# A gated recurrence with a convolution-gated linear unit: stores on ScalarE's queue, five output buffers, two x buffers, and gated inputs of two chunks from PSUM

## The chip, the cores and the metric

The kernel runs on one core of one Trainium2 chip. A core has five engines with a queue each: PE (TensorE, matrix products and transposes), DVE (VectorE), ACT (ScalarE, activation functions), POOL (GpSimd) and SP (SyncE, which here issues transfers). They share the on-chip memory SBUF; PE writes its results to the eight banks of PSUM, which DVE and ACT read. Transfers between HBM and SBUF are issued by an engine's queue and carried out by 16 DMA engines.

Each engine works through its own instructions in order and waits on semaphores where an operand, or a buffer to be overwritten, belongs to another engine. The metric is the device time of one execution in microseconds (us). The rows of the profile come from one profiled execution.

## The reference

Four sequences of 6336 tokens with 256 channels, all float32. First a gated linear recurrence over the tokens, then a linear unit whose gate is a causal convolution of the recurrence's output:

```python
sig_r = 1 / (1 + exp(-r_gate));  sig_i = 1 / (1 + exp(-i_gate))
a_t = exp(8 * sig_r * log(clip(sigmoid(a_param), 1e-6, 1 - 1e-6)))
x_gated = sqrt(maximum(1 - a_t * a_t, 1e-6)) * sig_i * x
for t in range(S):
    h = a_t[:, t] * h + x_gated[:, t];  y[:, t] = h
gate = 1 / (1 + exp(-sum_k(conv_w[k] * y_shifted_by(4 - k))))   # 5 taps
out = (gate * (y @ w_val)) @ w_out
```

## The kernel before

All 25,344 tokens are treated as one long row, cut into 28 chunks (`CHUNKS`, line 16): 256, 512, then 23 of 1024, then 512, 256 and 256. For the second half of the work a chunk is cut again into parts of at most 512 tokens, of which there are 51. In the plan an operation is named by its kind and by numbers: `tanh.7` is the tanh of chunk 7; `exp.7.1` belongs to chunk 7 and channel half 1; `conv.7.1` to chunk 7 and token part 1. A last number is the PSUM bank.

A chunk passes these steps; the line is the one that the profile shows:

- `ldri`, `ldx` (SP, L221 and L225): load r_gate and i_gate, and x. A gate buffer holds one chunk's pair, and there are three (`NRI`); there are three x buffers (`NX`).
- `tanh` (ACT, L294): tanh of half of both gates, in place as bf16.
- `srT` (PE, L299), `exp` (ACT, L308): transpose to channels on partitions, then the decay a, written to one of five slots of `aring`.
- `e` (POOL, L314): a squared. `sq` (ACT, L344): the square root of a quarter of 1 - a², for up to three chunks at once.
- `s1` and `u` (POOL, L322 and L335): one plus the tanh of the input gate, in place, then times x. For chunks 0 to 3 (`U_DVE`) DVE does both in one instruction per 256 tokens instead (L332), with the gate and x in SBUF.
- `nT` (PE, L357), `xg` (DVE, L364), `xgT` (PE, L372): transpose the root back, multiply the gated input by it, and transpose the product.
- `scan` (DVE, L385): the recurrence along the tokens of one channel half, into `yring`, which holds three chunks.
- `conv` (PE, L397), `tg` (ACT, L407), `val` (PE, L415), `gv` (DVE, L420), `out` (PE, L429): convolution, its tanh, value product, gating, output product.
- `osbD` (DVE, L444) or `osbA` (ACT, L440): the output from PSUM to one of three output buffers (`NOSB`).
- `store` (SP, L449): the output buffer to HBM.

The square root needs another activation table than tanh and exp, so ACT loads tables (ACT_TABLE_LOAD); before the change these loads come with the activations by themselves. Kernel set-up (L238 to L272) turns `a_param` into a scale, with an exponential between two logarithms on ACT, and turns the convolution weights into columns. `wd` (DVE, L279 and L280) makes from them the diagonal matrices of `conv`, and `wc` (DVE, L287 and L288) casts the two weight matrices. Their float32 originals, which `ldw` loads in five transfers on SP, lie in the last slot of `aring` until they are cast; chunk 4's exp writes that slot next.

The order is written out by hand in one string, `PLAN`. A loop runs through it and emits each operation to its engine, so the string sets the order on every queue. The loads that stand ahead of the first other operation are emitted before the set-up. SP carries loads and stores in one order: a load that stands behind a store in the plan is issued after it. Waits are added where buffers are shared.

Of the kernel before, what the change touches and what calls it, by code (L numbers as in the profile page):

```python
# [8 lines left out]
P = 128  # L9
HP = 64  # L10
SUBN = 512
BANK = 512
# [3 lines left out]
CHUNKS = [256, 512, 1024, 1024, 1024, 1024, 1024, 1024, 1024, 1024, 1024, 1024, 1024, 1024, 1024, 1024, 1024, 1024, 1024, 1024, 1024, 1024, 1024, 1024, 1024, 512, 256, 256]  # L16
U_DVE = [0, 1, 2, 3]
NRI = 3
NX = 3
# [4 lines left out]
NOSB = 3  # L24
# [9 lines left out]
ldri.1.-1 ldx.0.-1 ldri.0.-1 ldx.1.-1 tanh.1.-1 ldri.2.-1 tanh.0.-1 srT.1.0.5 exp.1.0.-1 srT.0.1.4 u.0.-1 srT.0.0.1  # L34
exp.0.0.-1 e.1.0.-1 u.1.-1 exp.0.1.-1 srT.1.1.1 exp.1.1.-1 e.0.1.-1 e.0.0.-1 e.1.1.-1 sq.0.1.-1 ldri.3.-1 sq.1.1.-1
tanh.2.-1 nT.1.0.5 xg.1.0.-1 xgT.1.0.7 nT.0.0.0 xg.0.0.-1 ldri.4.-1 xgT.0.1.6 scan.0.1.-1 tanh.3.-1 srT.2.1.4
srT.2.0.1 xgT.1.1.5 xgT.0.0.2 scan.0.0.-1 scan.1.1.-1 ldx.2.-1 exp.2.0.-1 wd.-1 srT.3.0.2 srT.3.1.5 exp.2.1.-1
e.2.0.-1 scan.1.0.-1 exp.3.1.-1 ldx.4.-1 e.2.1.-1 exp.3.0.-1 conv.0.0.4 tanh.4.-1 u.2.-1 e.3.0.-1 ldw.-1 ldx.3.-1
e.3.1.-1 tg.0.0.-1 srT.4.0.7 wc.-1 exp.4.0.-1 s1.4.-1 ldri.5.-1 sq.2.2.-1 val.0.0.6 srT.4.1.2 gv.0.0.-1 e.4.0.-1
u.3.-1 out.0.0.0 u.4.-1 osbD.0.0.-1 exp.4.1.-1 ldri.6.-1 nT.2.0.6 nT.2.1.0 xg.2.0.-1 nT.3.0.6 nT.3.1.4 tanh.5.-1  # L40
e.4.1.-1 xg.2.1.-1 xg.3.0.-1 xgT.2.1.5 xg.3.1.-1 conv.1.0.2 scan.2.1.-1 ldx.5.-1 tg.1.0.-1 srT.5.1.6 s1.5.-1 xgT.2.0.4
exp.5.1.-1 xgT.3.1.1 scan.2.0.-1 val.1.0.2 tanh.6.-1 e.5.1.-1 ldri.7.-1 scan.3.1.-1 srT.5.0.4 u.5.-1 conv.2.0.6
exp.5.0.-1 srT.6.1.5 gv.1.0.-1 conv.2.1.0 tg.2.0.-1 srT.6.0.3 ldx.6.-1 tg.2.1.-1 xgT.3.0.2 e.5.0.-1 exp.6.1.-1
scan.3.0.-1 val.2.0.0 exp.6.0.-1 ldri.8.-1 e.6.1.-1 tanh.7.-1 gv.2.0.-1 val.3.0.2 conv.3.0.4 e.6.0.-1 out.2.0.0
val.2.1.6 s1.6.-1 tg.3.0.-1 osbD.2.0.-1 sq.4.3.-1 gv.3.0.-1 ldx.7.-1 out.1.0.0 s1.7.-1 conv.3.1.4 osbD.1.0.-1
gv.2.1.-1 u.6.-1 srT.7.0.0 store.0.0.-1 store.1.0.-1 out.2.1.2 ldx.8.-1 osbD.2.1.-1 exp.7.0.-1 nT.4.0.1 u.7.-1
nT.4.1.2 xg.4.0.-1 ldri.9.-1 nT.5.0.7 xg.4.1.-1 srT.7.1.3 nT.5.1.1 xg.5.0.-1 tg.3.1.-1 nT.6.0.6 xgT.4.0.0 exp.7.1.-1
xg.6.0.-1 out.3.0.4 xg.5.1.-1 tanh.8.-1 val.3.1.2 osbD.3.0.-1 e.7.1.-1 xgT.5.0.6 gv.3.1.-1 xgT.5.1.5 store.2.1.-1
e.7.0.-1 scan.4.0.-1 nT.6.1.2 ldri.10.-1 srT.8.1.4 tanh.9.-1 srT.8.0.3 s1.8.-1 xgT.4.1.7 xg.6.1.-1 scan.4.1.-1 u.8.-1
exp.8.0.-1 scan.5.0.-1 conv.4.0.0 exp.8.1.-1 store.2.0.-1 conv.4.1.2 tg.4.0.-1 scan.5.1.-1 store.3.0.-1 srT.9.1.7  # L50
e.8.0.-1 val.4.0.0 exp.9.1.-1 ldx.10.-1 srT.9.0.4 tg.4.1.-1 gv.4.0.-1 xgT.6.0.5 e.9.1.-1 out.3.1.6 exp.9.0.-1
scan.6.0.-1 out.4.0.2 tanh.10.-1 ldx.9.-1 e.8.1.-1 val.4.1.0 osbD.3.1.-1 conv.5.0.4 e.9.0.-1 osbD.4.0.-1 ldx.11.-1
tg.5.0.-1 val.5.0.2 s1.9.-1 sq.7.3.-1 xgT.6.1.7 gv.5.0.-1 val.5.1.4 store.4.0.-1 gv.4.1.-1 out.5.0.2 s1.10.-1
store.3.1.-1 scan.6.1.-1 out.4.1.0 ldri.11.-1 u.9.-1 osbD.4.1.-1 conv.5.1.6 osbD.5.0.-1 tg.5.1.-1 nT.7.1.1 nT.7.0.0
xg.7.1.-1 srT.10.0.2 u.10.-1 xg.7.0.-1 srT.10.1.1 ldri.12.-1 exp.10.0.-1 xgT.7.0.0 gv.5.1.-1 conv.6.0.6 exp.10.1.-1
scan.7.0.-1 out.5.1.2 tg.6.0.-1 nT.8.0.1 tanh.11.-1 val.6.0.4 e.10.0.-1 xg.8.0.-1 osbD.5.1.-1 conv.6.1.6 gv.6.0.-1
store.4.1.-1 xgT.7.1.2 e.10.1.-1 val.6.1.0 scan.7.1.-1 store.5.0.-1 tg.6.1.-1 srT.11.0.3 srT.11.1.5 s1.11.-1
# [433 lines left out]
```

## Time and profile before

| | |
|---|---|
| median of 7 runs | 313.14 us (311.3 to 314.56) |
| the profiled execution | 311.45 us, of which the span from first to last instruction is 309.7 |
| busy: ACT | 281.4 us (91% of the span) |
| busy: DVE | 266.2 us (86%) |
| busy: PE | 245.3 us (79%) |
| busy: POOL | 230.7 us (74%) |
| moved by DMA | 104.76 MB, 338 GB/s over the span |
| granted clock of TensorE | 0.998 |

Rows of groups that the change touches (count, mean of one):

| line | engine and operation | count | mean ns |
|---|---|---|---|
| L332 | DVE, gated input, 128x512 | 11 | 1703 |
| L335 | POOL, gated input, 128x2048 | 21 | 4143 |
| L322 | POOL, one plus the gate, 128x2048 | 21 | 1919 |
| L314 | POOL, a squared, 128x1024 | 46 | 1947 |
| L444 | DVE, output copy, 128x1024 | 37 | 1213 |
| L440 | ACT, output copy, 128x1024 | 11 | 1008 |
| all | ACT_TABLE_LOAD | 24 | 1283 |

Busy time is the time in which an engine executes; a row's mean is that of one instruction, and neighbours on an engine overlap a little, so that the means add up to slightly more than the busy time. "Idle before, releaser" in a row says how long the engine stood idle ahead of an instruction and what ended that. An idle engine costs something only where it sets the pace.

### The profile page before, as it was taken

How to read it: one execution, taken by the hardware profiler on the slowest of the kernel's cores; microseconds unless marked ns; L12 is line 12 of the kernel's file. 1: busy time of each engine (PE TensorE's matmuls, PEld its weight loads, DVE VectorE, ACT ScalarE, POOL GpSimd, SP SyncE). 2: the span in 40 equal slices, each digit the busy share in tenths (PEclk: the TensorE clock that was granted, in tenths of full speed). 3: DMA queues.
4: the chain of work that ended last, by engine and by line, in shares of the span. 5: the costliest groups of instructions: out<-in, count | busy, mean ns of one | idle time of the engine just before them, and what ended most of it. 6: DMA issues, size and time to landing. Idle time of an engine off the chain costs nothing.

```text
span 309.7 us, 6478 instructions
## 1 busy us (share of the span) xinstructions
PE 245.3 (79%) x2655; PEld 167.9 (54%) x2655; DVE 266.2 (86%) x221; ACT 281.4 (91%) x191; POOL 230.7 (74%) x116
## 2 busy tenths in 40 slices
PE   0256156878868898979997998899979988999992
PEld 0134125546645665556765674657666655666561
DVE  1328978868798999999999999999999999889982
ACT  6999396999999999999999999999999998898652
POOL 0405985799899999997999699889999995690000
PEclk9999999999999999999999999999999999999999
DMA  7999655998999999999999999999999968563255
GB/s 268 421 424 382 259 247 223 431 380 297 372 424 416 377 380 416 390 424 369 392 362 359 323 426 419 423 424 341 354 416 398 357 239 336 196 217 134 103 205 205
DMA packets 20075, 104.76 MB, mean 338 GB/s; under 512 B 2247, under 2 KB 2766, under 8 KB 11214
## 3 DMA queue, kind: packets, MB, share of 16 engines
q1 hardware_dynamic: 20032, 104.34, 86.3%
q8 instruction: 21, 0.34, 0.4%
q14 instruction: 8, 0.07, 0.1%
q10 hardware_dynamic: 14, 0.01, 0.0%
HBM read 78.39 MB, written 25.95 MB: 337 GB/s over the span
## 4 chain that ended last, share of the span: by engine, by line
ACT 30%; DVE 30%; PE 16%; issue 16%; DMA 4%; POOL 1%; ACTq 0%; SPq 0%; DVEq 0%
DVE yring L385 11%; DVE gvr L420 8%; ACT gate L294 8%; ACT aring L308 7%; DVE osb L444 6%; ACT ering L344 6%; PE pp L397 5%; ACT tgr L407 4%; DVE uring L364 4%; PE pp L429 3%; DMA gate<-in_i_gate_dram 3%; PE pp L415 3%; PE pp L372 2%; PE pp L357 2%; ACT L344 2%
## 5 line engine op out<-in xcount | busy, mean ns | idle before, releaser
L314 POOL TENSOR_TENSOR ering<-aring 128x1024 f32<-128x1024 f32 (+2 forms) x56 | 97.2, 1756 | 35.7 <-ACT aring L308 35.5
L385 DVE TENSOR_TENSOR_SCAN yring<-aring,yring,pp 128x1024 bf16<-128x1024 f32 (+2 forms) x54 | 114.7, 2139 | 4.1 <-PE pp L372 4.1
L335 POOL TENSOR_TENSOR uring<-gate,xr 128x2048 bf16<-128x2048 bf16 (+2 forms) x24 | 91.2, 3813 | 5.0 <-DMA xr<-in_x_dram 4.7
L294 ACT ACTIVATE gate<-gate 128x4096 bf16<-128x4096 f32 (+2 forms) x28 | 90.3, 3230 | 1.6 <-DMA gate<-in_i_gate_dram 1.3
L397 PE MATMUL pp<-yring,diag 64*64 64x512 bf16 (+15 forms) x1260 | 66.9, 337 | 6.7 <-DVE yring L385 3.0
L420 DVE SCALAR_TENSOR_TENSOR gvr<-tgr,pp 128x1024 bf16<-128x1024 bf16 (+1 forms) x51 | 59.5, 1177 | 6.7 <-PE pp L415 3.5
L308 ACT ACTIVATE aring<-pp,khf 128x1024 f32<-128x1024 bf16 (+2 forms) x56 | 60.3, 1115 | 5.4 <-issue 5.1
L415 PE MATMUL pp<-yring,wv 128*128 128x512 bf16 (+1 forms) x204 | 51.0, 375 | 10.1 <-DVE wv L287 4.2
L407 ACT ACTIVATE tgr<-pp 128x1024 bf16<-128x1024 f32 (+1 forms) x51 | 50.8, 1004 | 8.3 <-PE pp L397 8.1
L429 PE MATMUL pp<-wo,gvr 128*128 128x256 bf16 x396 | 51.7, 275 | 4.9 <-DVE yring L385 2.0
L397 PEld LDWEIGHTS <-diag 64*64 64x64 bf16 x1260 | 32.5, 107 | 32.8 <-issue 17.1
L429 PEld LDWEIGHTS <-gvr 128*128 128x128 bf16 x396 | 42.0, 114 | 14.7 <-issue 8.2
L444 DVE COPY osb<-pp 128x1024 f32<-128x1024 f32 (+1 forms) x38 | 44.8, 1198 | 4.6 <-PE pp L429 3.5
L322 POOL TENSOR_SCALAR gate<-gate 128x2048 bf16<-128x2048 bf16 (+2 forms) x24 | 42.4, 1774 | 7.1 <-ACT gate L294 7.1
L344 ACT ACTIVATE ering<-ering,b 128x4096 bf16<-128x4096 f32 (+4 forms) x16 | 46.4, 2932 | 0.2
L357 PE MATMUL pp<-ident_f,ering 128*128 128x128 f32 x198 | 33.2, 309 | 15.3 <-ACT ering L344 9.1
L299 PE MATMUL pp<-ident_b,gate 128*128 128x128 bf16 x396 | 32.4, 233 | 16.0 <-ACT gate L294 12.5
L364 DVE TENSOR_TENSOR uring<-uring,pp 128x1024 bf16<-128x1024 bf16 (+1 forms) x51 | 32.4, 663 | 9.1 <-PE pp L357 8.2
L299 PEld LDWEIGHTS <-gate 128*128 128x128 bf16 x396 | 26.6, 104 | 25.1 <-ACT gate L294 15.9
L357 PEld LDWEIGHTS pp<-ident_f,ering 128*128 128x128 f32 x198 | 27.9, 208 | 20.9 <-ACT ering L344 11.8
L372 PE MATMUL pp<-ident_f,uring 128*128 128x128 f32 x198 | 32.5, 287 | 2.5 <-DVE uring L364 1.9
L415 PEld LDWEIGHTS <-wv 128*128 128x128 bf16 x204 | 19.4, 98 | 27.1 <-issue 9.4
(36 smaller groups left out, 93.1 us busy)
## 6 DMA issues: line engine op xcount, KB each, us to landing
out_dram<-osb SPq DMA_DIRECT2D x48, 512.0 KB, 5.8
gate<-in_r_gate_dram SPq DMA_DIRECT2D x23, 1024.0 KB, 8.9
gate<-in_i_gate_dram SPq DMA_DIRECT2D x23, 1024.0 KB, 9.3
xr<-in_x_dram SPq DMA_DIRECT2D x23, 1024.0 KB, 12.2
gate<-in_r_gate_dram SPq DMA_DIRECT2D x2, 512.0 KB, 4.6
gate<-in_i_gate_dram SPq DMA_DIRECT2D x2, 512.0 KB, 4.2
xr<-in_x_dram SPq DMA_DIRECT2D x2, 512.0 KB, 5.8
xr<-in_x_dram SPq DMA_DIRECT2D x3, 256.0 KB, 4.3
```

What stands on the lines that cost most here:

```text
L294: nc.scalar.activation(out=tgate[:, s0:s0 + 2, 0:w], in_=gate[:, s0:s0 + 2, 0:w], func=ACT.Tanh, scale=0.5)
L308: nc.scalar.activation(out=dst, in_=src, func=ACT.Exp, scale=khf[:, h:h + 1], bias=khf[:, h:h + 1])
L314: nc.gpsimd.tensor_tensor(out=ering[:, c % NE, h * n:(h + 1) * n], in0=a, in1=a, op=ALU.mult)
L335: nc.gpsimd.tensor_tensor(out=u, in0=t, in1=xt, op=ALU.mult)
L344: nc.scalar.activation(out=nring[:, c % NE:c % NE + m, 0:w], in_=ering[:, c % NE:c % NE + m, 0:w], func=ACT.Sqrt, scale=-0.25, bias=b025[: ...
L357: nc.tensor.transpose(out=pp[:, d0:d0 + P], in_=src[:, w, :], identity=ident_f[:])
L385: nc.vector.tensor_tensor_scan(out=yring[:, h, y0:y0 + n], data0=aring[:, c % NA, h, 0:n], data1=src, initial=prev, op0=ALU.mult, op1=ALU.add)
L397: nc.tensor.matmul(out=pp[col * HP:(col + 1) * HP, b0 + d0:b0 + d1], lhsT=diag[r * HP:(r + 1) * HP, h, kk, :], rhs=yring[r * HP:(r + 1) * ...
L415: nc.tensor.matmul(out=pp[:, (bank + m) * BANK:(bank + m) * BANK + n], lhsT=wv[:, hk, m, :], rhs=yring[:, hk, y0:y0 + n], start=(hk == 0), ...
L420: nc.vector.scalar_tensor_tensor(out=gvr[:, nth[k] % NGV, :, 0:n], in0=tgr[:, nth[k] % NTG, :, 0:n], scalar=1.0, in1=two(live["val", k], n ...
L429: nc.tensor.matmul(out=pp[:, bank * BANK + j * D:bank * BANK + (j + 1) * D], lhsT=gvr[:, nth[k] % NGV, m, 0:n].rearrange("c (p q) -> c q p ...
L444: nc.vector.tensor_copy(out=dst, in_=src)
```

## The change

- Chunks: 512, 23 of 1024, then 512, 512 and 256: 27 chunks and 50 parts.
- Stores are issued by ACT's queue, at places that the new plan sets, and there are five output buffers. There are two x buffers instead of three.
- For chunks 0 and 1 (`X_PE`) PE multiplies x by an identity matrix in float32 and so puts it into PSUM, 256 tokens at a time (`xc`), and DVE makes the gated input from there (`ux`; `u` is the last of them). Chunks 2 and 3 get `s1` and `u` on POOL as the later ones do.
- The diagonal matrices are made on POOL in the set-up. The weight casts are three instructions on ACT. The raw weights lie in the third chunk slot of `yring`, come in three transfers and are loaded ahead of everything but the first gates and x. The order of channels in the gated product changes (`QUADS`), and with it the way the casts and the load of `w_out` lay out their columns.
- Activation tables are loaded by name: a table with logarithm and exponential at the start, then the exponential one, and after that whenever the next of tanh, exp, tg and sq needs the other.
- The plan is a new one: 11 `sq` as before, in other groups (0; 1 and 2; 3 to 5; ...), 41 copies on DVE and 9 on ACT.

```diff
-CHUNKS = [256, 512, 1024, ..., 1024, 512, 256, 256]
-U_DVE = [0, 1, 2, 3]
+CHUNKS = [512, 1024, ..., 1024, 512, 512, 256]
+X_PE = [0, 1]
-NX = 3
+NX = 2
-NOSB = 3
+NOSB = 5
...
+ldri.0.-1 ldri.1.-1 ldx.0.-1 ldx.1.-1 ldri.2.-1 ldw.-1 tanh.0.-1 srT.0.0.7 srT.0.1.5 exp.0.1.-1 exp.0.0.-1 e.0.0.-1
+tanh.1.-1 e.0.1.-1 xc.0.1.0 xc.0.0.6 ux.0.0.-1 xc.1.2.1 u.0.-1 sq.0.1.-1 ux.1.2.-1 srT.1.0.0 ldri.3.-1 xc.1.1.5
+ldx.2.-1 nT.0.0.7 srT.1.1.4 exp.1.0.-1 xg.0.0.-1 ux.1.1.-1 exp.1.1.-1 xc.1.0.0 tanh.2.-1 xc.1.3.5 e.1.1.-1 ux.1.0.-1
+e.1.0.-1 wc.-1 srT.2.0.3 s1.2.-1 srT.2.1.2 xgT.0.0.4 exp.2.0.-1 scan.0.0.-1 exp.2.1.-1 e.2.0.-1 u.1.-1 tanh.3.-1
...
-        wvf = aring[:, NA - 1, 0, 0:H * D].rearrange("p (h n) -> p h n", h=H)
-        wof = aring[:, NA - 1, 1, 0:H * D].rearrange("p (h n) -> p h n", h=H)
+        wvf = yring[:, 0, 2 * CMAX:3 * CMAX].bitcast(FP32).rearrange("p (h n) -> p h n", h=H)
+        wof = yring[:, 1, 2 * CMAX:3 * CMAX].bitcast(FP32).rearrange("p (h n) -> p h n", h=H)
...
-        nc.scalar.activation(out=kln[:, 0:1], in_=b025[:], func=ACT.Ln)
+        nc.scalar.preload_act_table_set("natural_log_exp_and_others")
...
+        nc.scalar.preload_act_table_set("exp_and_others")
...
-        def op_wd(k, bank):
-            nc.vector.tensor_tensor(out=id64[:], ...
+        nc.gpsimd.tensor_tensor(out=id64[:], in0=ident_f[:, 0:HP], in1=ident_f[:, HP:P], op=ALU.add)
+        nc.gpsimd.tensor_tensor(out=diag[:].rearrange("p h k m -> p (h k) m"), ...
...
         def op_wc(k, bank):
+            for hk in range(H):
+                nc.scalar.copy(out=wv[:, hk, :, :].rearrange("p m (i c) -> p i m c", i=2),
+                               in_=wvf[:, hk, :].rearrange("p (i m c) -> p i m c", i=2, m=2))
+            nc.scalar.activation(out=wo2[:], in_=wof, func=ACT.Copy, scale=0.5)
...
+        def op_xc(k, bank):
+            c, w = k
+            nc.tensor.matmul(out=pp[:, bank * BANK:(bank + 1) * BANK], lhsT=ident_f[:],
+                             rhs=xr[:, c % NX, 2 * w:2 * w + 2, :].rearrange("p b d -> p (b d)"),
+                             start=True, stop=True)
+
+        def op_ux(k, bank):
+            c, w = k
+            u, t = gated(c)
+            b = live["xc", k]
+            nc.vector.scalar_tensor_tensor(out=u[:, w], in0=t[:, w], scalar=1.0,
+                                           in1=pp[:, b * BANK:(b + 1) * BANK].rearrange("p (b d) -> p b d", b=2),
+                                           op0=ALU.add, op1=ALU.mult)
...
-        QUADS = ((0, 0, 0), (0, 1, 1), (1, 0, 1), (1, 1, 0))
+        QUADS = ((0, 0, 0), (0, 1, 1), (1, 1, 1), (1, 0, 0))
...
-            nc.sync.dma_start(toks(of, c, o, n),
-                              osb[:, nth[k] % NOSB, 0:n // P * D].rearrange("p (q d) -> p q d", d=D))
+            nc.scalar.dma_start(toks(of, c, o, n),
+                                osb[:, nth[k] % NOSB, 0:n // P * D].rearrange("p (q d) -> p q d", d=D))
...
+            if o[0] in ("tanh", "exp", "tg", "sq"):
+                want = "sqrt_and_others" if o[0] == "sq" else "exp_and_others"
+                if want != table:
+                    nc.scalar.preload_act_table_set(want)
+                table = want
```

On ACT the new plan begins `tanh.0 exp.0.1 exp.0.0 tanh.1 sq.0.1 exp.1.0 exp.1.1 tanh.2 wc exp.2.0 exp.2.1 tanh.3 sq.1.2 exp.3.1 tanh.4 tg.0.0 exp.3.0 exp.4.1 tanh.5 tg.1.0 exp.4.0 exp.5.1 exp.5.0 tanh.6 tg.1.1 store.0.0 tg.2.0 sq.3.3`, and ends `sq.25.2 tg.22.1 osbA.21.1 store.20.0 tg.23.1 store.21.1 tg.23.0 store.20.1 store.22.1 store.22.0 tg.24.0 osbA.23.0 store.23.1 tg.25.0 store.23.0 tg.26.0 store.24.0 osbA.25.0 store.25.0 osbA.26.0 store.26.0`.

## The prediction

> **What bounds the kernel now.** I first read the busy times by stretch (per engine: us busy, instructions; then the granted clock, the DMA share, GB/s).
>
> ```profile
> core 0: us, PE busy (x) PEld busy (x) DVE busy (x) ACT busy (x) POOL busy (x), PEclk, DMA share, GB/s
> 0.00:8.00 8.00, 0.60 (x3) 0.46 (x3) 1.02 (x7) 5.64 (x7) 0.70 (x6) 1.00 0.77 273
> 8.00:40.00 32.00, 12.36 (x86) 8.55 (x87) 19.19 (x20) 26.43 (x20) 15.85 (x9) 1.00 0.95 374
> 40.00:80.00 40.00, 29.17 (x310) 20.12 (x310) 31.44 (x26) 36.93 (x23) 34.14 (x13) 1.00 0.81 317
> 80.00:180.00 100.00, 88.22 (x961) 60.35 (x959) 96.85 (x74) 99.33 (x59) 92.86 (x43) 1.00 0.99 385
> 180.00:260.00 80.00, 71.10 (x783) 49.58 (x782) 78.81 (x61) 79.42 (x49) 73.07 (x34) 1.00 0.97 380
> 260.00:280.80 20.80, 20.65 (x235) 13.40 (x233) 18.40 (x16) 18.10 (x22) 14.05 (x12) 1.00 0.55 202
> 280.80:309.70 28.90, 23.22 (x288) 15.44 (x284) 20.51 (x20) 15.58 (x18) 0.00 (x0) 0.98 0.42 165
> ```
>
> From 80 to 260 ACT is busy 178.75 us of 180 and DVE 175.66: a pair sets the pace. The DMA share of 0.97 to 0.99 is a queue that is never empty, not a bound: in the waits of the compute engines, gate loads cost ACT 1.3 us and x loads POOL 4.7 in the whole run. After 280.8, the end of the last square root, PE is full and the rest is a tail. So time can come from the first 80 us (ACT idle 11.0, DVE 28.3) and the tail.
>
> The largest hole of ACT, in the timeline (start, us, engine):
>
> ```profile
> 36.49 2.30 DVE L287 CAST wv<-aring 128x128 bf16<-128x128 f32 x4
> 38.72 0.41 DVE L288 TENSOR_SCALAR wo<-aring 128x512 bf16<-128x512 f32 x1
> 38.88 1.20 ACT L308 ACTIVATE aring<-pp,khf 128x1024 f32<-128x1024 bf16 x1 [5.12 <-issue]
> ```
>
> "Issue" hides the reason. This exp writes the decay slot in which the raw weights lie, and their casts stand on DVE behind chunk 2's gated inputs. Those are slow for a reason that one line shows (min/median/max):
>
> ```profile
> L332 DVE SCALAR_TENSOR_TENSOR uring<-gate,xr x11: 706/1234/4622, 11.0 to 47.7; 128x512 bf16<-128x512 bf16 x11
> ```
>
> The same shape takes 706 ns or 4622; the long one lies over POOL's 4.56 us multiply at 42.0. Both its tensors are in SBUF.
>
> **The change, part by part.** Span 309.7, the execution 311.45, so 1.75 lies around it; the median of seven is 313.14, 1.0054 times that execution. I carry span to time by both.
>
> *Gated inputs.* Chunks 0 and 1 (1536 tokens) stay on DVE: 6 pieces instead of 11. With x in PSUM the nearest row is L420's 128x512 form, one operand in SBUF and one in PSUM: 678 ns; bounds 0.68 and the 1.70 mean of before. I take 0.68, for one SBUF operand is what that row has: 4.1 us against 17.9, and 3.9 of idling go. PE gains six fp32 products 512 wide: four times L357's 0.309, 1.2 each, 7.4 us, at 9 to 20 where PE is mostly idle. Chunks 2 and 3 add two s1 (1.92) and two u (4.14) to POOL, +12.1; with `diag` there too (0.8 as on DVE to 1.5 at POOL's rate for e), and e no longer slowed from 1.9 to 2.4 beside DVE's pieces, POOL comes to 230.7+12.1+1.8-1.9-0.9 (one chunk fewer), about 242. From the first e at 10 to 276 it has 266.
>
> *Casts.* DVE loses 2.7 us, and 1.0 of `op_wd`. ACT gains three copies: 0.4 to 0.59 each, from below the 128x512 copy of L440 (585 ns); I take 1.5. The staging moves into y's third slot, so the wait of 5.1 goes; next is the scan of chunk 2, far later.
>
> *Order of the four convolution quarters:* as many matmuls as before, at the same array positions; nothing.
>
> *Tables.* Start: two loads fewer, so the first tanh begins when data land: loads issued at 0.73 and 1.18, landing after 3.3 and 4.2, so 5.4 instead of 8.08. But there are eleven square-root phases for ten: two loads of 1.283 more. The total stays 24; nothing gained but an earlier start.
>
> *Chunks and copies.* One chunk of 512 for two of 256 saves ACT 1.2 and DVE 0.7. ACT's output copies go from 13 to 9: -3.6; DVE's from 38 to 41: +4.9.
>
> *Stores.* On SP a store's wait holds the loads behind it:
>
> ```profile
> SPq L449 <- DVE osb L444: 71.9, 20, 7.5
> SPq L449 <- ACT osb L440: 28.7, 11, 5.8
> L449 SPq DMA_DIRECT2D out_dram<-osb x51: 332/344/2007, 64.0 to 305.3; - x51
> ```
>
> [...] By the rows SP stood 100.6 us at stores, yet the late loads cost at most 1.3+4.7=6.0. I take 0: PE and DVE are near full under those waits.
>
> The cost is on ACT: 50 issues at 344 ns, 17.2 us if bare, 0 if under a running activation. The only rows on ACT's own queue are two small loads at 0.54 and 0.27. On run-ahead:
>
> ```profile
> L407 ACTq EVENT_SEMAPHORE  x45: 17/17/5316, 59.4 to 301.2; - x45
> ACT tgr L407 <- PE pp L397: 8.1, 8, 2.9
> ```
>
> ACT's queue stood 5.3 us at a wait while the engine never idled over 2.9 before tg, so it was at least 2.4 us ahead. [...] I take 1.3. A store whose copy is late holds every tanh, exp, tg and square root behind it, and through them all engines; but the new order puts most stores several ACT instructions after their copy.
>
> *Five output buffers, two x buffers.* The chain of waits ends so:
>
> ```profile
> 300.31 1.02 ACT osb L440
> 301.35 3.24 DMA out_dram<-osb
> ...
> 304.69 0.58 ACT osb L440
> ```
>
> It promises 3.2 us. But the last out product only ends at 304.57, so the buffer wait costs 0.1. With two x buffers, x of chunk c waits for u of c-2. In POOL's new order seven such gaps (after u of 2, 5, 8, 11, 14, 17, 20) hold two s1, two e, one u: 2x1.92+2x1.95+4.14=11.9 us, against a median landing of 12.2. I charge 1.0.
>
> **Two clocks and the sum.** ACT: before, 265.85 busy and 14.95 idle up to 280.8. After, total 281.45-3.6-1.2-0.2+1.5=277.95, of which 10.0 follow the last square root (five tg at 0.95, one at 0.55, four copies, a load), so 268. Idle: 2.5 before the first tanh, 0.3 behind the first transposes, and before's later 0.67+0.58+2.70; the 2.9 before 54 (tg of chunk 1 behind conv) I count as gone, for conv of chunk 1 no longer follows DVE's slow pieces. 268+6.75=274.7. Tail: of PE's work queued behind the last root, a 512-token part costs 1.24 (conv), 0.86 (val) and 0.87 (out) in the chain of waits and a transposed half 0.6. Before has, in 512s, 5.5 conv, 6 val, 8 out and 4 halves: 21.6 us with small ones; after 3.6, 5.5, 7.5 and 1.5: 16.9. So the tail is 28.9-4.7=24.2. ACT's clock: 298.9.
>
> DVE: total 266.2-13.8-3.7+4.9-0.7=252.9. When is it fed without holes? ACT's new order, each at its row's mean (tanh 3.6, exp 1.2, tg 1.0, square root 3.7 for two chunks, load 1.28): first tanh to 7.4, exps 9.9, tanh 1 13.5, load, square root 0 and load 17.2, exps 19.6, tanh 2 23.2, casts 24.7, exps 27.1, tanh 3 30.7, load, square roots 1 and 2, load 37.0, then exp, tanh 4, tg, two exps, tanh 5, tg, three exps, tanh 6, two tg: 59.0. Load and square roots 3 and 4: 64.0. POOL keeps up: the last e that roots 1 and 2 need ends at 29.8 against 30.7. The transposes and PE take 1.3 more, so from 65.3 DVE is fed, with 4.1 of pieces, 1.2 of set-up, 3.4 of gating, 11.9 of scans and 9.6 of five gv and five copies done, 30.2: 222.7 left. Before had 224.8 left at 65.3, and then idled 19.6: 4.5 up to 80, then 3.15, 1.19, 2.4 and, in the tail, 8.4. After I keep all but the 4.5 and 2 of the tail: 13.1. 65.3+222.7+13.1=301.1.
>
> The later clock counts: 301.1+1.3+1.0=303.4 span, 305.2 the execution, **307.0** as a median.
>
> **Rivals.** *A, stores stall ACT* (the slower side). Place: ACT's queue between 60 and 270, where ACT is full. Bare issues give 301.1+17.2=318.3, **322**. It decides from 0.17 us a store on, where 50 eat the 8.6 gained. For it: ACT has no slack, and one issue of before took 2.0 us. Against it: the run-ahead. *B, two x buffers starve POOL.* If x comes 3 us late in seven gaps (landings of before reached 15.6), 21 us; POOL's spare is 24 less some 10 at the start, so 7 come through: 301.1+1.3+7=309.4, **313**. Against it: with the stores off SP, x loads are issued as soon as u ends. *C, the lead is lost to DVE.* The casts and the slow pieces lay where DVE waited anyway, and the new order idles as the old did: 65.3+222.7+19.6=307.6, **311.0**. For it: DVE's work left at 65 shrinks by only 2 us. *D, the named table preloads do not replace the automatic loads*: 24x1.283=31 more, **345**.
>
> **How the numbers follow.** Forecast 0.55, A 0.22, B 0.09, C 0.11, D 0.03. (C's figure lies at the edge of no change.) Half a per cent is about what these runs can tell from no change: 311.6 and 314.7. Faster: the forecast and part of C, 0.61; same: the rest of C, most of B and a little of A, 0.15; slower: A mainly, D, some B, 0.24. The forecast's own range is 302 to 311: DVE's tail idle gone altogether, or C's hole half kept. Half of A (8.6 bare) is 309.7, or 313.1 as a median; reaching 8 in 10 takes the top to 317.
>
> **What would show it.** First tanh near 5.5; no idle before exp of chunk 3 or 4; six pieces near 0.7 us; about 24 table loads; square roots 3 to 5 done near 66 (before: 4 to 6 at 76.2); ACT still above 99% to 260; the last square root near 276. Wrong if ACT shows holes after 60 with a store ahead of them in its queue, if POOL waits for x by more than 10 us, or if DVE falls under 95% after 80.

## The result, and the profile after

The changed kernel takes 310.28 us (median of 12 runs, 308.98 to 311.06), the kernel before 313.14: a ratio of 0.9903, with a 95% interval from 0.9884 to 0.9923. That is faster by 2.9 us, where 6.1 were forecast. The profiled execution took 309.9 us, of which the span is 307.8. Here and below, the few executions that took over 1.5% more than the fastest of their kernel are left out of the medians.

Busy time by stretch, in the same columns as before; the last root now ends at 284.2:

```profile
core 0: us, PE busy (x) PEld busy (x) DVE busy (x) ACT busy (x) POOL busy (x), PEclk, DMA share, GB/s
...
8.00:40.00 32.00, 18.70 (x91) 11.81 (x91) 8.03 (x11) 30.03 (x20) 20.55 (x10) 0.75 1.00 401
40.00:80.00 40.00, 31.03 (x363) 21.34 (x362) 32.60 (x27) 39.47 (x24) 37.50 (x18) 0.99 0.97 376
80.00:180.00 100.00, 84.52 (x908) 57.72 (x906) 91.84 (x72) 95.86 (x59) 93.36 (x42) 0.98 0.98 391
180.00:260.00 80.00, 71.55 (x794) 49.79 (x791) 79.15 (x63) 78.64 (x49) 71.21 (x34) 1.00 0.84 327
260.00:284.20 24.20, 21.89 (x250) 13.44 (x246) 21.82 (x16) 18.80 (x22) 9.35 (x9) 1.00 0.46 174
284.20:307.80 23.60, 19.16 (x240) 12.80 (x230) 17.66 (x18) 10.51 (x11) 0.84 (x1) 0.99 0.53 212
```

Three stretches matter. From 8 to 40 ACT gained 3.6 us of work over before, and from 40 to 80 another 2.5: the early holes are gone. The tail after the last root is 23.6 us instead of 28.9. But between 80 and 180, where ACT had been busy 99.33 us of 100, it now has 95.86. One hole makes almost all of that. ACT alone, in the timeline (start, us, engine; an "ACTq" row is the queue's own work, the issue of a store):

```profile
142.53 1.25 ACT L304 ACTIVATE aring<-pp,khf 128x1024 f32<-128x1024 bf16 x1
143.62 1.08 ACT L417 ACTIVATE tgr<-pp 128x1024 bf16<-128x1024 f32 x1
148.19 0.34 ACTq L459 DMA_DIRECT2D out_dram<-osb  x1
148.65 3.62 ACT L290 ACTIVATE gate<-gate 128x4096 bf16<-128x4096 f32 x1 [3.96 <-DMA xr<-in_x_dram]
```

The tanh of chunk 15 (L290) is said to have waited 3.96 us for x. It doesn't read x. What stands between it and the activation before it is a store, of chunk 8's first part, issued at 148.19. That part's copy had ended at 142.6. The load that the row names is that of x of chunk 14 (L224, first the issue, in ns and at which us; then from issue to landing):

```profile
L224 SPq DMA_DIRECT2D xr<-in_x_dram x1: 375/375/375, 135.3 to 135.3; - x1
...
DMA to landing us min/median/max: 12.8/12.8/12.8
```

It landed at 148.1, just before the store was issued. The next store, of chunk 8's second part, was issued at 150.91, and the load of x of chunk 15 had landed at 150.8 (issued at 142.84, 8.0 us to landing). ACT's queue has a semaphore record right ahead of each of these two stores, at 148.1 and 150.9. By these times each of the two stood until a load had landed that it doesn't read; what ties it to that load the trace does not show. The input gate of chunk 15 had landed at 144.4, 9.6 us after its issue at 134.8, so the tanh itself could have started then. Both waits are nothing that the computation needs.

A second place is at the end. In the chain of work that ended last (start, us, what was waited for or done), a load of x and the issue of a store both stand as links:

```profile
142.85 7.99 DMA xr<-in_x_dram
...
270.44 1.76 ACTq L459
```

There three stores were issued in 2.62 us, one of them in 1.76, and the two exps behind them started after 1.65 us of idle time, though their transposes had ended by 271.3. This is not a wait like the first: the long issue is that of the second store (chunk 18's first part), and ACT's queue has no semaphore record ahead of any of the three (L459, 268.8 to 272.6). Why it took 1.76 us is open. Elsewhere between 66 and 250 ACT has no hole behind a store: the other issues ran under activations.

The stores' row, all on ACT's queue (ns of one, min/median/max), and DVE's pieces from PSUM:

```profile
L459 ACTq DMA_DIRECT2D out_dram<-osb x50: 338/339/1759, 56.9 to 304.9; - x50
```

```profile
L335 DVE SCALAR_TENSOR_TENSOR uring<-gate,pp x6: 706/726/737, 16.0 to 28.2; 128x512 bf16<-128x512 bf16 x6
```

### The profile page after: what moved, and what is told of

Same layout as the page of the kernel before. It is cut to its first block, busy times and chain, and to the rows that moved or that the text cites. A ratio compares the mean times of both kernels' runs of the same rounds, so it can differ in the third digit from the quotient of the medians.

```text
span 307.8 us, 6335 instructions
## 1 busy us (share of the span) xinstructions
PE 247.6 (80%) x2627; PEld 167.5 (54%) x2627; DVE 252.2 (82%) x208; ACT 278.2 (90%) x185; POOL 235.1 (76%) x118
## 4 chain that ended last, share of the span: by engine, by line
PE 30%; DVE 23%; DMA 14%; ACT 14%; issue 12%; POOL 3%; ACTq 2%; SPq 1%; DVEq 0%
DVE yring L395 13%; PE pp L407 8%; PE pp L439 7%; DMA gate<-in_i_gate_dram 6%; DMA xr<-in_x_dram 6%; PE pp L425 5%; DVE gvr L430 5%; ACT tgr L417 4%; PE pp L367 4%; DVE osb L454 4%; ACT aring L304 3%; ACT gate L290 3%; DMA out_dram<-osb 3%; POOL uring L345 3%; PE pp L327 2%
## 5 line engine op out<-in xcount | busy, mean ns | idle before, releaser
L310 POOL TENSOR_TENSOR ering<-aring 128x1024 f32<-128x1024 f32 (+2 forms) x54 | 93.6, 1752 | 35.7 <-ACT aring L304 35.5
L395 DVE TENSOR_TENSOR_SCAN yring<-aring,yring,pp 128x1024 bf16<-128x1024 f32 (+2 forms) x52 | 113.4, 2193 | 3.7 <-PE pp L382 3.7
L345 POOL TENSOR_TENSOR uring<-gate,xr 128x2048 bf16<-128x2048 bf16 (+2 forms) x25 | 96.1, 3847 | 4.2 <-PE pp L382 2.6
L290 ACT ACTIVATE gate<-gate 128x4096 bf16<-128x4096 f32 (+2 forms) x27 | 90.2, 3342 | 6.7 <-DMA xr<-in_x_dram 4.0
L407 PE MATMUL pp<-yring,diag 64*64 64x512 bf16 (+13 forms) x1224 | 65.1, 340 | 5.9 <-DVE yring L395 2.5
L304 ACT ACTIVATE aring<-pp,khf 128x1024 f32<-128x1024 bf16 (+2 forms) x54 | 59.2, 1144 | 3.8 <-PE pp L295 2.0
L417 ACT ACTIVATE tgr<-pp 128x1024 bf16<-128x1024 f32 (+1 forms) x50 | 50.5, 1024 | 10.0 <-PE pp L407 8.6
L454 DVE COPY osb<-pp 128x1024 f32<-128x1024 f32 x41 | 49.0, 1210 | 5.7 <-PE pp L439 5.6
L318 POOL TENSOR_SCALAR gate<-gate 128x2048 bf16<-128x2048 bf16 (+2 forms) x25 | 44.4, 1779 | 5.4 <-ACT gate L290 5.4
L407 PEld LDWEIGHTS <-diag 64*64 64x64 bf16 x1224 | 30.4, 107 | 31.2 <-issue 14.8
L295 PE MATMUL pp<-ident_b,gate 128*128 128x128 bf16 x396 | 31.1, 229 | 13.2 <-ACT gate L290 10.8
L367 PE MATMUL pp<-ident_f,ering 128*128 128x128 f32 x198 | 32.3, 303 | 4.8 <-ACT ering L354 3.9
```

The lines of the kernel that those rows point to most:

```text
L290: nc.scalar.activation(out=tgate[:, s0:s0 + 2, 0:w], in_=gate[:, s0:s0 + 2, 0:w], func=ACT.Tanh, scale=0.5)
L304: nc.scalar.activation(out=dst, in_=src, func=ACT.Exp, scale=khf[:, h:h + 1], bias=khf[:, h:h + 1])
L310: nc.gpsimd.tensor_tensor(out=ering[:, c % NE, h * n:(h + 1) * n], in0=a, in1=a, op=ALU.mult)
L345: nc.gpsimd.tensor_tensor(out=u, in0=t, in1=xt, op=ALU.mult)
L367: nc.tensor.transpose(out=pp[:, d0:d0 + P], in_=src[:, w, :], identity=ident_f[:])
L395: nc.vector.tensor_tensor_scan(out=yring[:, h, y0:y0 + n], data0=aring[:, c % NA, h, 0:n], data1=src, initial=prev, op0=ALU.mult, op1=ALU.add)
```

## The experiments

Each ratio is to executions of the kernel before on the same chip; their medians lie between 313.1 and 314.3 us from chip to chip.

**All stores back on SP (e1), and once more (e14).** The order is that of the changed kernel.

```diff
-            nc.scalar.dma_start(toks(of, c, o, n),
+            nc.sync.dma_start(toks(of, c, o, n),
```

> The changed kernel with its 50 stores issued by SP again, at the same places of the order. In the changed kernel's trace ACT shows no idle time ahead of an instruction that a store precedes, except 1.65 us at 272.7 behind three store issues. Theory 1 (a store on ACT's queue is issued under the running activation, so it costs ACT nothing, and moving it off SP brings SP's loads little): within 2 us of the changed kernel's 310.3, that is 308.5 to 312.5; ACT's busy time from 80 to 220 stays above 98%. Rival (the stores on ACT cost about 0.1 us each, or about 2 us at 272): faster, about 307. Second rival (on SP the waits of the stores for their copies hold the loads of gates and x, and the move is what pays): slower, 313 or more, with new idle time of ACT ahead of tanh or of POOL ahead of u, released by a load.

> The changed kernel with all its stores on SP once more, beside the two mixed ones on the same chip: 304.2 as the first time, within 1 us, by every theory.

Measured: 304.19 us, ratio to before 0.971 (0.9681 to 0.974); the second time 304.54, 0.9731 (0.9686 to 0.9777). By the ratios, 0.971 and the changed kernel's 0.9903, the stores on ACT cost 1.9% or 6 us. The theory that they cost nothing fell; it had passed over the 3.96 us, which the row puts down to x. The gain is also larger than either rival had it. Busy time by stretch with stores on SP:

```profile
core 0: us, PE busy (x) PEld busy (x) DVE busy (x) ACT busy (x) POOL busy (x), PEclk, DMA share, GB/s
80.00:180.00 100.00, 85.98 (x952) 59.08 (x950) 94.14 (x72) 98.65 (x59) 95.81 (x44) 1.00 0.99 398
180.00:260.00 80.00, 70.99 (x758) 49.42 (x757) 79.44 (x63) 78.95 (x52) 68.66 (x32) 1.00 0.87 331
260.00:279.70 19.70, 19.29 (x227) 11.86 (x230) 17.88 (x14) 15.83 (x19) 9.49 (x9) 1.00 0.50 193
279.70:303.30 23.60, 19.26 (x246) 12.89 (x234) 18.19 (x19) 10.51 (x11) 0.70 (x1) 1.00 0.48 190
```

ACT is back at 98.65 us of 100, the last root ends at 279.7 instead of 284.2, and the tail is the same 23.6. On SP the stores wait as they did there before the change (the queue's own waits: us in all, times, longest):

```profile
SPq L459 <- DVE osb L454: 43.7, 12, 7.4
SPq L459 <- ACT osb L450: 16.6, 5, 7.1
```

These are 60 us of waiting, with loads queued behind it, and the compute engines hardly show it: ACT waits 2.0 us in all for gates (2.6 in the changed kernel), DVE 2.3 us for output buffers.

**Two places of the order altered, stores on ACT (e5).**

```diff
-store.8.0.-1 tanh.15.-1
+tanh.15.-1 store.8.0.-1
-store.18.1.-1 ... store.18.0.-1 store.19.0.-1 ... exp.25.0.-1 out.20.0.4 exp.26.0.-1
+exp.25.0.-1 out.20.0.4 exp.26.0.-1 store.18.1.-1 store.18.0.-1 store.19.0.-1
```

They are the places of the 3.96 and the 1.65 us.

> The changed kernel, stores on ACT as it has them, with two places of the order altered: the store of chunk 8's first part stands behind the tanh of chunk 15 instead of ahead of it, and the three stores ahead of the last two exps of channel half 0 stand behind them. The sequence of transfers stays the same. [...] Rival (the cost lies in the 50 issues, or in loads and stores on two queues sharing the transfer engines): less than 1.5 us faster, 309 or more, or new holes in the same place.

Measured: 307.28 us, ratio 0.9787 (0.9739 to 0.9836), 3.0 us under the changed kernel by medians and 3.6 by ratios: less than the 5.6 us of the two holes, and well over the rival's 1.5. ACT in the timeline:

```profile
144.93 3.68 ACT L289 ACTIVATE gate<-gate 128x4096 bf16<-128x4096 f32 x1
148.53 0.34 ACTq L458 DMA_DIRECT2D out_dram<-osb  x1
149.00 1.02 ACT L416 ACTIVATE tgr<-pp 128x1024 bf16<-128x1024 f32 x1 [0.38 <-PE pp L424]
151.13 0.34 ACTq L458 DMA_DIRECT2D out_dram<-osb  x1
151.50 1.28 ACT L471 ACT_TABLE_LOAD   x1 [1.48 <-DVE gvr L429]
```

The tanh of chunk 15 starts at 144.93 without a wait: its own data were there. The store still waits until 148.5, now under the tanh, where it costs at most the 0.38 us ahead of the next activation. But the next store, issued at 151.13 after x of chunk 15 had landed at 150.8, now has the square root's table load behind it, and a hole of 1.48 opens there. This shows the mechanism of the first place: what matters is what stands behind a store that waits. At the second place the two exps now start after 0.16 us of idle time instead of 1.65, and the copy behind the moved stores after 0.65.

**That store moved as well (e9).** It now stands behind `sq.12.3`. Of the gap to the stores on SP, 307.28 - 304.19 = 3.1 us remain after e5.

> As the run with two places of the order altered, stores on ACT, and with one more: the store of chunk 8's second part stands behind the square root of chunks 12 to 14 instead of ahead of it. In that run ACT had a new hole of 1.48 us at 150.0, right behind that store's issue at 151.13, when x of chunk 15 had just landed at 150.8. [...] Rival (what remains is a cost of each issue, or of two transfer queues beside each other): within 0.7 us of 307.3.

Measured: 306.93 us, 0.9788 (0.9756 to 0.982). The hole at 150 is gone and the span is 304.9 instead of 305.9, but the medians hardly differ (307.28 and 306.93): the rival's band holds. In this trace a copy at 271.04 starts 1.05 us late behind issues of 0.82 us for two and 0.79 for one, and the tanh of chunk 25 waits 1.39 us for its gate instead of 0.65 with the stores on SP. Beside the profiled execution with all stores on SP (e1) this one is 1.6 us longer in its span: that tanh starts 0.64 us later (250.60 against 249.96) and that copy 1.50 (271.04 against 269.54).

**Where the rest of the cost lies (e12, e13).** The same order, with the stores split between the queues by chunk:

```diff
-            nc.scalar.dma_start(toks(of, c, o, n),
+            (nc.scalar if c < 17 else nc.sync).dma_start(toks(of, c, o, n),
```

and with `c >= 17` for the other.

> The order with the three moved places, stores of chunks 0 to 16 issued by ACT and those of chunks 17 to 26 by SP. Theory 1 (what is left of the stores' cost lies at the end: issues that stand bare ahead of the last exps and copies, 1.05 us at 271, and the gates of chunk 25 that come 0.7 us later): within 1 us of the kernel with all stores on SP, about 304 to 305. Rival (a cost of each issue or of two queues, spread over the run): 33 of 50 stores, so about 306.

> The same order, stores of chunks 17 to 26 issued by ACT and the earlier ones by SP. Theory 1: nearly as slow as with all on ACT in this order, 306 to 307. Rival (spread over the run): 17 of 50 stores, about 305.

Measured on one chip: early stores on ACT 305.41 (0.9756, from 0.9719 to 0.9792), late ones on ACT 307.33 (0.9798, from 0.9745 to 0.9851), none on ACT, in the changed kernel's own order, 304.54. The medians lie as the first theory has them, 0.9 and 2.8 us above, but the intervals overlap and the runs of the second reach from 305.0 to 309.2. So the end of the run is the likelier place of the remainder, as the two traces beside each other have it too; by the times it is not settled.

**Three output buffers (e3 on ACT, e6 on SP) and three x buffers (e4 on ACT, e8 on SP).** Thirteen stores stand earlier in the order, most of them eight to eleven places ahead of the copy that needs their buffer; in e4 and e8 `ldx` stands right behind `ldri`.

```diff
-NOSB = 5
+NOSB = 3
```

```diff
-NX = 2
+NX = 3
```

> The changed kernel with three output buffers instead of five; 13 of the 50 stores stand earlier in the order, as three buffers need it. Theory 1 (five buffers buy little, since the output copies do not wait for buffers): within 1 us of the changed kernel's 310.3. Rival (five buffers are what lets the stores stand several instructions behind their copies on ACT, and with three the stores stall ACT): slower by 2 us or more, with idle time of ACT behind a store.

> Stores on SP, and three output buffers instead of five with the 13 stores moved earlier as in the run on ACT that took 354 us. Theory 1 (that run was slow because stores on ACT's queue that wait for a transfer hold ACT, and the two extra buffers only let the stores stand far behind in ACT's order): within 1.5 us of the run with stores on SP and five buffers, 303.5 to 306. Rival (three buffers are too few for this order on any queue, output copies on DVE wait for stores): 315 or more, with DVE waiting for stores in its copies by over 10 us (44.4 us in the run that took 354).

> The same kernel with three output buffers as in the run before (two buffers make room for one), and with three x buffers instead of two; each chunk's x is loaded right behind its gates, so that it waits for the gated input of three chunks earlier and no longer for that of two chunks earlier. Theory 1 (with two x buffers SP stood with all buffers full from 86 to 96 us, the transfers went slack at 259 GB/s there, and the lag came back as 3.96 us in which ACT waited for chunk 15's input gate at 144.7): the hole at 144.7 goes, no wait of ACT for a gate over 1 us between 70 and 240, and the time falls by 2.5 to 4 us against the run with three output buffers alone, to about 306.5 to 308. Rival (the transfers run at 96% of their rate on the whole and the third buffer only moves the wait elsewhere; or the DVE sets the time and takes the hole up): the time stays within 1 us of the run with three output buffers alone.

> As the run with three output buffers and stores on SP, and with three x buffers instead of two, each chunk's x loaded right behind its gates. Theory 1 (two x buffers cost what the prediction charged, about 1 us): 0.5 to 1.5 us faster than three output buffers on SP alone. Rival (they cost nothing, since POOL waits for ACT and PE and not for x): within 0.5 us.

Measured: 353.64 (e3), 345.02 (e6), 356.12 (e4) and 351.01 us (e8); the ratios are 1.1285, 1.0992, 1.1347 and 1.1182. My own theory failed in all four; the slower rivals of e3 and e6 came true. The queue isn't what makes three buffers slow: on SP they cost 41 us too. The waits of the output copies for stores, on ACT's queue (e3):

```profile
DVE osb L453 <- DMA out_dram<-osb: 44.4, 15, 6.9
```

and on SP's, with three x buffers (e8):

```profile
DVE osb L453 <- DMA out_dram<-osb: 42.7, 11, 8.7
```

DVE stands for over 40 us at buffers that are still being stored. In the changed kernel no such row is among its waits, and with five buffers on SP it is 2.3 us. So few places of the order are too short for a transfer that takes 5.4 us in the median (e3; 6.5 in e8); stores placed closer behind the copies that fill their buffers were not tried, so this shows that this order needs the five buffers, not that no order could do with three. For the same reason the third x buffer is not judged by these runs; the stall of ACT that I had first put down to two x buffers goes away in e1 with two.

**Gated inputs from x in SBUF (e2).** The six products that copy x are left out, and DVE reads x directly.

```diff
-                                           in1=pp[:, b * BANK:(b + 1) * BANK].rearrange("p (b d) -> p b d", b=2),
+                                           in1=xr[:, c % NX, 2 * w:2 * w + 2, :],
```

> The changed kernel without the six fp32 products that copy x of chunks 0 and 1 into PSUM: DVE reads x from SBUF instead. Theory 1 (the pieces lie where DVE waits anyway, so their length does not count unless chunk 0's or 1's gated input comes after its root): pieces grow from 0.72 us to 1 to 2 us where POOL's multiplies run beside them, 4 to 8 us more of DVE busy before 40 us, and the time stays within 1.5 us of the changed kernel's 310.3. Rival (DVE's work is the clock all along): slower by the growth, 314 to 318. PE has 8.6 us less work before 24 us; if the granted clock of 0.50 at 24 to 42 us comes from PE standing idle, it stays low there or is low earlier.

Measured: 311.15 us, 0.9927 (0.9901 to 0.9953), against 0.9903 with them: no difference that these runs can tell. The pieces took 714 to 1282 ns, with a median of 728; from PSUM it is 726. Only one grew: five of the six lie where POOL stands idle. The sixth lies over POOL's squares of chunk 2. From SBUF (e2):

```profile
28.05 1.28 DVE L333 SCALAR_TENSOR_TENSOR uring<-gate,xr 128x512 bf16<-128x512 bf16 x1
26.85 4.20 POOL L309 TENSOR_TENSOR ering<-aring 128x1024 f32<-128x1024 f32 x2 [0.23 <-ACT aring L303]
```

and from PSUM, in the changed kernel:

```profile
28.21 0.71 DVE L335 SCALAR_TENSOR_TENSOR uring<-gate,pp 128x512 bf16<-128x512 bf16 x1
27.01 3.74 POOL L310 TENSOR_TENSOR ering<-aring 128x1024 f32<-128x1024 f32 x2 [0.23 <-ACT aring L304]
```

There x in PSUM spares DVE 0.57 us and POOL 0.46. It is one piece, and the time doesn't show it. The other five are as fast from SBUF (728 ns is the median of all six); POOL's work no longer lies over them.

**The hole of 5.12 us alone, in the kernel before (e7).** The raw weights go into y's third slot; order and casts stay.

```diff
-        wvf = aring[:, NA - 1, 0, 0:H * D].rearrange("p (h n) -> p h n", h=H)
-        wof = aring[:, NA - 1, 1, 0:H * D].rearrange("p (h n) -> p h n", h=H)
+        wvf = yring[:, 0, 2 * CMAX:3 * CMAX].bitcast(FP32).rearrange("p (h n) -> p h n", h=H)
+        wof = yring[:, 1, 2 * CMAX:3 * CMAX].bitcast(FP32).rearrange("p (h n) -> p h n", h=H)
```

> The kernel before with one thing altered: the raw weights wait for their casts in the third slot of y instead of in the last slot of the decay's ring; order and casts as before. Theory 1, as in the prediction (the exp of chunk 4 no longer waits 5.12 us behind casts on DVE; ACT's start sets when DVE is fed): the hole at 33.8 to 38.9 goes and the end comes 2 to 4 us earlier, 309 to 311. Rival, as in the prediction's case C (the early lead is lost where DVE is the clock): the hole goes, roots 4 to 6 end some 4 us earlier than 76.2, and the time stays within 1 us of 313.1.

Measured: 315.46 us, 1.0039 (1.0003 to 1.0076): no gain, if anything a loss. DVE in the timeline of this run:

```profile
28.43 8.16 DVE L332 SCALAR_TENSOR_TENSOR uring<-gate,xr 128x512 bf16<-128x512 bf16 x4
36.49 7.94 DVE L287 CAST wv<-yring 128x128 bf16<-128x128 f32 x4
```

The exp that waited 5.12 us starts 4.5 us earlier. POOL's next square and its multiply of chunk 4 then start earlier too, at 38.29 and 40.14, and lie over the casts, which take 7.94 us for four instead of 2.30; TensorE waits behind them, and ACT gets two holes of 4.07 and 4.95 us. So this run does not test the hole alone.

**The casts on ACT as well (e15).** The two instructions of `op_wc` are issued on `nc.scalar` instead of `nc.vector`.

```diff
-                    nc.vector.tensor_copy(out=wv[:, :, m, i * HP:(i + 1) * HP], in_=wvf[:, :, lo:lo + HP])
-            nc.vector.tensor_scalar(out=wo2[:], in0=wof, scalar1=0.5, scalar2=None, op0=ALU.mult)
+                    nc.scalar.copy(out=wv[:, :, m, i * HP:(i + 1) * HP], in_=wvf[:, :, lo:lo + HP])
+            nc.scalar.activation(out=wo2[:], in_=wof, func=ACT.Copy, scale=0.5)
```

> The kernel before with the raw weights in y's third slot and, other than in the run with that alone, the casts on ACT at their old place of the order (five short ACT instructions, about 2 us). The casts on DVE had grown from 2.30 to 7.94 us beside POOL's squares, and TensorE stood 9.5 us behind them. Theory 1, as in the prediction (ACT's wait of 5.12 us goes and what follows comes earlier): no hole over 1 us before 46 us, roots 4 to 6 end 2 us or more before 76.2, and the time falls by 1 to 4 us to 309 to 312. Rival, as in case C (DVE and its slow gated inputs set the pace in the old order): another hole of ACT opens before 60 us, roots 4 to 6 end within 1 us of 76.2, and the time stays within 1 us of 313.1.

Measured: 313.05 us, 0.9989 (0.9949 to 1.0029), no difference. The next wait takes the place of the one removed; ACT and, from the same stretch, DVE:

```profile
53.43 1.02 ACT L407 ACTIVATE tgr<-pp 128x1024 bf16<-128x1024 f32 x1 [6.22 <-PE pp L397]
```

```profile
37.51 10.52 DVE L332 SCALAR_TENSOR_TENSOR uring<-gate,xr 128x512 bf16<-128x512 bf16 x4
```

Chunk 3's four gated inputs, at 2.6 us each beside POOL's squares and multiply, hold up the output copy behind them on DVE. The transposes that stand ahead of the convolution of chunk 1 on TensorE wait 6.29 us for that copy. Roots 4 to 6 end at 75.54, 0.6 us before those of the kernel before.

**Their gated inputs on POOL as well (e16).** Chunks 2 and 3 get `s1` and `u` on POOL, still in the old order.

```diff
-U_DVE = [0, 1, 2, 3]
+U_DVE = [0, 1]
-u.2.-1
+s1.2.-1 u.2.-1
-u.3.-1
+s1.3.-1 u.3.-1
```

> As the run before, with the gated inputs of chunks 2 and 3 on POOL (two more of 1.9 and two more of 4.1 us there) instead of eight slow pieces on DVE, in the kernel before's order. Theory 1 (the slow pieces are what held the convolution of chunk 1, and with it ACT, for 6.22 us at 47.2): that hole shrinks under 2 us, roots 4 to 6 end at 71 to 74 instead of 75.5, and the time falls by 1 to 4 us to 309 to 312. Rival (the old order makes POOL's added 12 us the next wait, ahead of the squares that the roots need): roots 4 to 6 end later than 75.5 and the time is 313 or more.

Measured: 315.45 us, 1.0072 (1.0041 to 1.0103), 0.7% slower. The hole before the convolution's tanh shrinks to 0.57 us, but ACT's square root of chunks 2 and 3 now waits 3.25 us for POOL, whose queue has chunk 2's product ahead of chunk 3's squares:

```profile
30.88 1.89 POOL L322 TENSOR_SCALAR gate<-gate 128x2048 bf16<-128x2048 bf16 x1
32.86 4.10 POOL L335 TENSOR_TENSOR uring<-gate,xr 128x2048 bf16<-128x2048 bf16 x1
36.90 3.75 POOL L314 TENSOR_TENSOR ering<-aring 128x1024 f32<-128x1024 f32 x2
```

Three parts of the change, made one after the other in the old order, bring nothing: each hands the wait to another engine. In the new order nearly the same tokens have their roots at 66.23, 7.4 us earlier (76.18 - 66.23, less 2.6 for 256 tokens). What in that order does it was not taken apart further.

**Four copies of the tail on ACT, stores on SP (e10).** `osbD` becomes `osbA` for 22.1, 22.0, 23.1 and 24.0.

> Stores on SP, and four output copies of the tail (both parts of chunk 22, one of 23, chunk 24) on ACT instead of DVE: 4.9 us less for DVE, 4.0 us more for ACT after 280 us. In the tail of the run with stores on SP ACT is busy 10.2 us of 23.3 and DVE 17.9. Theory 1 (DVE is the clock to the end, as in the prediction's sum): 1 to 3 us faster than the 304.2 of stores on SP. Rival (the tail is a chain through PE, ACT and DVE in turn, and a copy costs the same on either): within 0.7 us.

Measured: 304.68 us, 0.9737 (0.9696 to 0.9779), no gain over e1. The tail by stretch:

```profile
280.00:302.00 22.00, 17.92 (x223) 11.96 (x221) 12.62 (x13) 12.71 (x14) 0.00 (x0) 0.97 0.51 204
```

DVE is busy 12.62 us of 22 there and nothing is won: DVE isn't the clock of the tail. PE, at 17.92, is the fullest.

**Idle TensorE filled at the start, stores on SP (e11).** 48 products that nobody reads are added.

```diff
+            for _ in range(k[0]):
+                nc.tensor.matmul(out=pp[:, bank * BANK:bank * BANK + 2 * P], lhsT=ident_b[:],
+                                 rhs=ident_f[:].bitcast(BF16), start=True, stop=True)
```

> Stores on SP, and 48 products of the identity with itself, whose results nobody reads, in TensorE's three idle stretches between 22 and 37 us. With stores on SP 16 transposes took 1.9 us at 24.6 and 16 fp32 ones 4.0 us at 36.6, as long as in the run without the fp32 products; the recorded clock there was 0.50. Theory 1 (the short work finds TensorE slow after it stood idle, and DVE's first product of chunk 2 waits for it): the 16 fp32 transposes take about 2.4 us, DVE starts 1.5 us earlier at 37.8, and the time falls by 0.5 to 1.5 us against 304.2. Rival (the start is set by ACT, whose activations follow each other without holes there): the transposes get shorter and the time stays within 0.5 us.

Measured: 305.59 us, 0.9742 (0.9715 to 0.9768). Sixteen transposes took 1.07 us instead of 1.9 and the sixteen fp32 ones some 2.5 instead of 4.0 (last section), and the end did not come earlier: ACT, busy 17.94 us of the 18 from 24 to 42 with the products and without, has no hole there. The median is 1.4 us above e1's, taken on another chip, which neither theory has.

## Why the prediction was right or wrong

**The step that failed** is the stores' cost on ACT, "I take 1.3". No run shows that term, which was my estimate between the two bounds; the runs show 6.1 us by medians in its place (310.28 against 304.19). The spans of the two profiled executions, 307.8 and 303.3, give 4.5, because the one with stores on SP was the slowest of its six. The bounds, 0 to 17.2, held it; the reason for going low did not. "The new order puts most stores several ACT instructions after their copy" looked at one wait of a store only, that for its copy. The wait that cost most, 3.96 us at one store, is the one until x of chunk 14 had landed, which neither the source nor the trace of before shows as such. The second place, 1.65 us, shows no such wait: three issues in a row, one of them of 1.76 us, stood bare ahead of the exps. For that there was a sign: the prediction named the issue of 2.0 us in before, for rival A, and still took 1.3 for all 50 in the sum. The run-ahead I argued from is real (2.4 us in the trace of before), but it hid short issues of 0.34 us, not a wait and not the long issue. Moving the stores at these places (e5, e9) gave back 3.0 to 3.4 of the 6.1 us; the rest lies most likely at the end of the run and is not settled.

**Rival A** was the right mechanism at a third of its price: 6.1 us over 50 stores is 0.12 each, under the 0.17 from which it was to decide. It is not spread over the stores as its sum had it, either: 5.6 us of ACT's idle time stand at two places.

**The two clocks.** ACT was busy 278.16 - 10.51 = 267.65 us up to its last root; 268 was forecast. Its idle time there was 284.2 - 267.65 = 16.5 instead of 6.75. Of the difference 5.6 are the two stalls behind stores; the start took 5.4 us of holes (1.60, 0.64 and 0.70 before the first tanh, 1.13 and 0.40 behind transposes, 0.50 and 0.47 for gates) where 2.5, 0.3 and 0.67 were counted. With stores on SP it is 11.7. The tail was 23.6 against 24.2, right. The sum then used DVE's clock, as the later one. That choice is not borne out: in e10 DVE lost 4.9 us of tail work without effect, and in the changed kernel, e1 and e9 alike the end comes 23.6 us after ACT's last root. It did little harm to the figure, because the two clocks lay close: e1's span is 303.3, and the forecast without its charge for stores is 302.1. Two small slips are in the sum's text: 303.4 + 1.75, times 1.0054, is 306.8 and not 307.0, and PE, called full in the tail of before, is busy 23.22 us of 28.90 there.

**Right in size:** square roots 3 to 5 done at 66.23 (66); DVE 252.2 us busy (252.9) and ACT 278.2 (277.95); 24 table loads; the pieces at 0.726 us each (0.68); casts 1.42 (1.5). The first tanh started at 5.91 (5.4). The products that copy x took 8.6 us (7.4), beside idle time as forecast. POOL's growth was over-charged: it was busy 235.1 (242), 4.4 us more than before instead of 11.

**Right in sign, partly wrong in reason:** the pieces are fast, but five of the six not for having x in PSUM; the one beside POOL's squares is (0.71 us against 1.28, e2). The 5.12 us hole went, but taken away in the old order it was worth nothing (e15), nor with the slow gated inputs gone too (e16): there rival C is right. It does not describe the changed kernel: with stores on SP the lead of 7.4 us at the roots near 66 is 8.3 at those near 220 (219.22 against 230.14, less 2.6 for 256 tokens), and the spans still differ by 6.4 at the end (303.3 against 309.7).

**Mis-charged:** two x buffers, 1.0; POOL waited for x 0.8 us in the whole run, so nearly nothing. Five output buffers, a buffer wait that "costs 0.1": the tail shows no more, but the new order depends on them (e3, e6).

**Of the signs named,** "ACT still above 99% to 260" failed, and "ACT shows holes after 60 with a store ahead of them in its queue" came true; so did DVE under 95% after 80 (91.84 of 100). DVE waited 3.8 us there for a tanh of ACT that was queued behind the stalled store; but with the stores on SP it is 94.14, so the stall is not all of it.

The version that beats both kernels is the changed one with its stores on SP: 304.2 and 304.5 us.

## What to carry to other kernels

Before a transfer is moved onto the queue of the engine that sets the pace, list everything its issue can wait for, and look at what stands behind it: here a store stood until a load had landed that it doesn't read. An issue of 0.34 us that didn't wait was hidden under the running activation here, one that waited held the engine for 3.96 us, and three issues in a row held it for 1.65. When a row says that an instruction waited for data it doesn't read, look at the queue entry ahead of it. A hole in the bounding engine is worth its length only if what comes next on the other engines is ready earlier too (the 5.12 us here were worth nothing in e15); removing it alone in the old order is a cheap way to see what comes next.

## What the runs showed of the hardware

**In these runs the recorded clock of TensorE does not show that it starts slow.** Sixteen bf16 transposes and then the fp32 ones of chunk 2's roots, in the changed kernel:

```profile
24.65 1.89 PE L295 MATMUL pp<-ident_b,gate 128*128 128x128 bf16 x16 [2.70 <-ACT gate L290]
...
36.60 3.96 PE L367 MATMUL pp<-ident_f,ering 128*128 128x128 f32 x16 [2.71 <-ACT ering L354]
```

with x read from SBUF (e2):

```profile
24.49 1.89 PE L294 MATMUL pp<-ident_b,gate 128*128 128x128 bf16 x16 [5.13 <-ACT gate L289]
...
36.45 3.84 PE L365 MATMUL pp<-ident_f,ering 128*128 128x128 f32 x16 [2.71 <-ACT ering L352]
```

and with the filled idle time (e11), where the second group is shown in two:

```profile
24.41 1.07 PE L294 MATMUL pp<-ident_b,gate 128*128 128x128 bf16 x16 [1.39 <-ACT gate L289]
...
36.25 1.23 PE L371 MATMUL pp<-ident_f,ering 128*128 128x128 f32 x8 [1.13 <-ACT ering L353]
37.85 1.23 PE L371 MATMUL pp<-ident_f,ering 128*128 128x128 f32 x8 [0.37 <-DVE uring L378]
```

The first two run at the same pace, but the granted clock of 24 to 42 us is 0.53 in one and 1.00 in the other (after, then e2):

```profile
24.00:42.00 18.00, 10.02 (x73) 7.65 (x74) 5.52 (x7) 17.94 (x12) 17.68 (x8) 0.53 0.99 400
```

```profile
24.00:42.00 18.00, 10.18 (x76) 8.35 (x77) 6.10 (x7) 17.54 (x12) 17.69 (x8) 1.00 0.91 365
```

In the changed kernel eight transposes at 7.88 us took 1.04 us, and eight at 17.41, behind 5.29 us of the products that copy x, took 0.61; the recorded clock is 1.00 at both and falls to 0.50 from 24 to 26 us. In e2, without these products, eight transposes took 1.03 at 14.91 and 1.06 at 18.30, and the record stays at 1.00. So in this early stretch the duration of a known instruction told more than the recorded clock. When TensorE becomes slow again is not settled here: after 2.70 us of idle time the transposes at 24.65 took 1.89 us in the changed kernel, while in e11 those at 31.23, after 2.91 us, still took 1.07.

**A store's issue is not always 0.34 us.** Of three in a row on ACT one took 1.76 (at 270), with no semaphore record ahead of it in ACT's queue; on SP the longest was 2.0 in the kernel before. What makes an issue long was not found.
